# Decode attention: 256 rows of wo loaded to the lower half of the partitions through eight DMA engines, and O turned to match

## The chip, the cores and the metric

One core of one Trainium2 chip. The metric is the device time of one execution, in microseconds (us). Where single executions are compared I also give their span, the time from the first to the last instruction. All runs here are of state fast. The granted clock is the share of TensorE's full clock that the profile records, and half clock is 0.5. SBUF is the on-chip memory in which the tiles here lie, on 128 partitions; PSUM holds TensorE's results (`s_ps`, `acc`). Names: PE is TensorE's matmul, PEld its weight load, DVE VectorE, ACT ScalarE, SPq the queue of SyncE that issues the loads.

## The reference

Attention over a cache for one new token, plus an MLP, on a normalised input:

```python
B, Sq, D = 8, 1, 576;  H, Sk, Dh = 32, 4096, 128;  F = 4608
xn = layernorm(x)
q  = (xn @ wq) as [B, H, 1, Dh]
o  = softmax(q @ k_cache^T * Dh**-0.5) @ v_cache      # caches: 8 x 32 x 4096 x 128, bf16
return x + o as [B, 1, H*Dh] @ wo + gelu(layernorm(xn) @ w1 + b1) @ w2 + b2
```

The two caches are 537 MB; wo is 4096 x 576 (4.7 MB) and w2 is 4608 x 576 (5.3 MB).

## The kernel before

32 tiles of K and 32 of V stream through a ring in SBUF, 8.4 MB each. While the last tile is computed, w2 and then wo are queued behind it. The tail does the second layer of the MLP (`hidden_part`, twice 18 row blocks), turns the attention output into OT, and multiplies it by the 32 rows of wo that each partition holds.

```python
CUTS = (0, 12, 23, 30, RO)                      # RO = 32 rows of wo per partition
...                                             # SyncE, after two blocks of the last K tile
sy.dma_start(out=w2_sb..., in_=w2_v).then_inc(w2_in, 16)
wo_in = []
for n, (r0, r1) in enumerate(zip(CUTS, CUTS[1:])):
    if n == 1:
        sy.wait_ge(sem["kf"], NX * (NT - 1) + 5)
    wo_in.append(nc.alloc_semaphore(f"in_wo{n}"))
    to, rows = wo_rows(r0, r1), wo_v[:, r0 * D:r1 * D]
    sy.dma_start(out=to, in_=rows).then_inc(wo_in[-1], 16)
...                                             # TensorE, the tail
te.wait_ge(w2_in, 16)
hidden_part()                                   # 18 row blocks, two matmuls each (a "pair")
te.wait_ge(sem["on"], NT)
... # 8 matmuls: S_ps[0] <- Ox, low
hidden_part()
te.wait_ge(sem["on"], NT + 1)                   # VectorE has copied OT out of PSUM
for n, (r0, r1) in enumerate(zip(CUTS, CUTS[1:])):
    te.wait_ge(wo_in[n], 16)
    rows = wo_rows(r0, r1).rearrange("p (r d) -> p r d", d=D)
    for r in range(r0, r1):
        ins = accumulate(te, OT[:, r, :], rows[:, r - r0, :], stop=(r == RO - 1))
ins.then_inc(sem["end"], 1)
```

`accumulate` is a pair: two matmuls of 288 columns, into two PSUM banks.

The softmax here doesn't subtract the row's maximum and nothing guards it: scores larger than these inputs give would overflow.

Of the kernel before, what the change touches and what calls it, by code (L numbers as in the profile page):

```python
# [4 lines left out]
ACT = mybir.ActivationFunctionType  # L5
# [3 lines left out]
BF16 = mybir.dt.bfloat16  # L9
P = 128  # L10
# [113 lines left out]
def decode(nc, A_x, A_k_cache, A_v_cache, A_wq, A_wo, B_x, B_w1, B_b1, B_w2, B_b2, out):  # L124
    B, _, D = A_x.shape
# [5 lines left out]
    NT = B * NHG  # L131
# [14 lines left out]
    RO = HD // P  # L146
# [12 lines left out]
    wo_v = A_wo.rearrange("(p r) d -> p (r d)", r=RO)  # L159
    k_v, v_v = (c.rearrange("b h (p c) d -> (b h p) (c d)", p=QP) for c in (A_k_cache, A_v_cache))  # L160

    def sb(name, shape, dtype):
        return nc.alloc_sbuf_tensor(name, list(shape), dtype)

    TILE = 2 * CHUNK
    BLOCK = CB * Dh
    NX = 2 * NCB
    RING = 3 * TILE - BLOCK
    ring = sb("ring", [P, RING], BF16)[:]
# [9 lines left out]
    on = sb("on", [P, G], BF16)  # L179
    fin = sb("fin", [P, ND], BF16)  # L180
    OT = sb("OT", [P, RO, B], BF16)
    hT_sb = sb("hT_sb", [P, R, 2 * B], BF16)
    ident = sb("ident", [P, P], BF16)
    ones_b = sb("ones_b", [1, B], BF16)
# [17 lines left out]
    def early(room, shape, dtype=BF16):  # L202

        n = 2 if dtype == FP32 else 1
        for m in shape[1:]:
            n *= m
        a = rooms[room][0]
        rooms[room][0] = a + (n + 15) // 16 * 16
        assert rooms[room][0] <= rooms[room][1]
        t = ring[:shape[0], a:a + n]  # L210
        if dtype == FP32:
            t = t.bitcast(FP32)
        if len(shape) > 2:
            names = "abcd"[:len(shape) - 1]
            t = t.rearrange(
                f"p ({' '.join(names)}) -> p {' '.join(names)}", **dict(zip(names, shape[1:])))
        return t
# [10 lines left out]
    q = early(0, [P, NB])  # L228
# [10 lines left out]
    S_ps = [s_all[:, i * NB:(i + 1) * NB] for i in range(NS)]  # L239
# [4 lines left out]
    sem = {n: nc.alloc_semaphore(f"m_{n}") for n in names}  # L244
# [23 lines left out]
    def home(t, kind):  # L268

        return 0 if kind else TILE + t % 2 * (TILE - BLOCK)  # L270

    def load_kv(cache, t, kind):
# [10 lines left out]
        out=ident[:], in_=ident[:], compare_op=ALU.not_equal, fill=1.0, base=0,  # L283
# [11 lines left out]
    def act(reads, writes, emit):  # L295
        return od.op("scalar", reads, writes, emit)
# [19 lines left out]
    def spread(src, skey, p0):  # L316
# [5 lines left out]
        out=par2[:], in_=ident[:].rearrange("p (u v) -> p v u", v=2), axis=AX.X, op=ALU.add))  # L322
    dve(["par2"], ["par"], lambda e: e.tensor_copy(
        out=par[:, 0::2], in_=par2[:].unsqueeze(1).to_broadcast([P, (WC + 1) // 2, 2])))
    for v in range(2):
        dve(["par2"], ["par"], lambda e: e.tensor_copy(
            out=par[:, 1::2, v:v + 1],
            in_=par2[:, 1 - v:2 - v].unsqueeze(1).to_broadcast([P, WC // 2, 1])))
# [3 lines left out]
    idn = ident[:]  # L332
# [10 lines left out]
    for t, (dst, dkey) in enumerate(((xT, "xT"), (yT, "yT"))):  # L343
        for v in range(2):
            dve(["tot", "par"], [dkey], lambda e: e.tensor_tensor(
                out=dst[:, :, v * B:(v + 1) * B], in0=tp[:, :, t],
                in1=par[:, :, v:v + 1].to_broadcast([P, WC, B]), op=ALU.mult))
    act(["ident"], ["sel"], lambda e: e.activation(
        func=ACT.Copy, out=sel, in_=idn.rearrange("p (m i) -> p i m", m=M)[:, :2 * B, :].unsqueeze(3)
        .to_broadcast([P, 2 * B, M, QP])))  # L350
    dve(["ident"], ["selc"], lambda e: e.tensor_reduce(
        out=selc[:], in_=idn.rearrange("p (m g c) -> p c g m", m=M, c=4), axis=AX.X, op=ALU.add))
    dve(["ident"], ["headf"], lambda e: e.tensor_reduce(
        out=headf[:], in_=idn.rearrange("p (g q) -> p g q", g=G), axis=AX.X, op=ALU.add))
    act(["headf"], ["head"], lambda e: e.activation(out=head[:], in_=headf[:], func=ACT.Copy))
    with nc.allow_low_precision(reason="zeros and ones"):
        dve(["ident"], ["quad"], lambda e: e.tensor_reduce(
            out=quad[:], in_=idn.rearrange("p (m r) -> p m r", m=M), axis=AX.X, op=ALU.add))
        dve(["ident"], ["low"], lambda e: e.tensor_reduce(
            out=low[:], in_=idn.rearrange("p (m r) -> p r m", m=M), axis=AX.X, op=ALU.add))  # L360
    act(["ident"], ["bv"], lambda e: e.activation(
        func=ACT.Copy, out=bv[:, :2 * B].rearrange("p (v b) -> p v b", v=2),
        in_=ident[:2, :2].unsqueeze(2).to_broadcast([2, 2, B])))


    def queries(e):
        for c in range(WC):
            wv = wq_sb[:, c, :].rearrange("p (x m d) -> p m x d", m=M, d=Dh)
            for m in range(M):
                i = e.matmul(  # L370
                    S_ps[0][m * MP:(m + 1) * MP, :], lhsT=xT[:, c, :], rhs=wv[:, m],
                    start=(c == 0), stop=(c == WC - 1))
        return i

    def accumulate(e, lhsT, rhs, start=False, stop=False):
        for m in range(NO):
            i = e.matmul(  # L377
                acc[m][m * OP:m * OP + B, :ND], lhsT=lhsT, rhs=rhs[:, m * ND:(m + 1) * ND],
                start=start, stop=stop)
        return i  # L380
# [44 lines left out]
    for j in range(HJ):  # L425
        t1, k1, hp, h = t1s[j], f"t1_{j}", h_ps[j], hs[j]
        act(["h_ps"], [k1], lambda e: e.activation(out=t1, in_=hp, func=ACT.Square))  # L427
        dve([k1], [k1], lambda e: e.tensor_scalar(  # L428
            out=t1, in0=t1, scalar1=0.044715, scalar2=1.0, op0=ALU.mult, op1=ALU.add))
# [3 lines left out]
            out=t1, in0=t1, scalar1=1.0, scalar2=0.5, op0=ALU.add, op1=ALU.mult))  # L433
        dve([k1, "h_ps"], [f"h{j}"], lambda e: e.tensor_tensor(
            out=h, in0=t1, in1=hp, op=ALU.mult))
    for j in range(HJ):
        h = hs[j]
        t = S_ps[j][:, :HK * HS * MP].rearrange("p (k n) -> p k n", k=HK)

        def turn(e, h=h, t=t):  # L440
# [8 lines left out]
            out=hT_sb[:].rearrange("p (s j k) n -> p j k s n", s=HS, j=HJ)[:, j],  # L449
            in_=t.rearrange("p k (s n) -> p k s n", s=HS)[:, :, :, :2 * B]))  # L450
# [1 line left out]
    mlp_done = [od.last(e) for e in ("tensor", "vector", "scalar")]  # L452


    CUTS = (0, 12, 23, 30, RO)
    W2_AT = home(NT, 0)
    WO_AT = (W2_AT + 2 * R * D, home(NT - 1, 0))
    assert WO_AT[0] + CUTS[1] * D <= WO_AT[1] and (RO - CUTS[1]) * D <= 3 * BLOCK
    w2_sb = ring[:, W2_AT:WO_AT[0]].rearrange("p (v r d) -> p v r d", v=2, d=D)

    def wo_rows(r0, r1):
        at = WO_AT[0] + r0 * D if r0 < CUTS[1] else WO_AT[1] + (r0 - CUTS[1]) * D
        return ring[:, at:at + (r1 - r0) * D]

    sy = nc.sync
    for token in (wq_read, *head_done):
        od.wait("sync", token)
# [10 lines left out]
    sy.dma_start(out=w2_sb.rearrange("p v r d -> p v (r d)"), in_=w2_v).then_inc(w2_in, 16)  # L478
    wo_in = []
    for n, (r0, r1) in enumerate(zip(CUTS, CUTS[1:])):  # L480
        if n == 1:
            sy.wait_ge(sem["kf"], NX * (NT - 1) + 5)
        wo_in.append(nc.alloc_semaphore(f"in_wo{n}"))
        to, rows = wo_rows(r0, r1), wo_v[:, r0 * D:r1 * D]
        sy.dma_start(out=to, in_=rows).then_inc(wo_in[-1], 16)
    sy.br("sync_end").branch_hint(sync_last)


# [15 lines left out]
    ve, sa, te = nc.vector, nc.scalar, nc.tensor  # L504
# [87 lines left out]
    with nc.Fori(0, NT // 2, 1, engines=[ENG.DVE, ENG.Activation]) as it:  # L592
# [8 lines left out]
    ve.tensor_copy(  # L601
        out=OT[:], in_=S_ps[0][:, :RO * B].rearrange("p (r b) -> p r b", b=B)).then_inc(sem["on"], 1)
    ve.wait_ge(sem["end"], 2)
    ve.tensor_copy(out=fin[:B], in_=acc[0][:B, :ND]).then_inc(fin_d, 1)  # L604
    sa.wait_ge(sem["end"], 2)
    sa.activation(
        out=fin[OP:OP + B], in_=acc[1][OP:OP + B, :ND], func=ACT.Copy).then_inc(fin_a, 1)
    sa.wait_ge(fin_a, 1)
# [34 lines left out]
    def value(name, low, high):  # L643
        return te.snap(regs[name].handles[0], min_val=low, max_val=high)
# [3 lines left out]
    to = s_all[:, bass.ds(value("bank", 0, (NS - 1) * NB), NB)].rearrange("p (c d) -> p c d", d=DL)  # L648
    te.wait_ge(sem["prod"], 1).then_inc(sem["prod"], -1)  # L649
    for d in range(Dh // DL):  # L650
        ins = te.matmul(  # L651
            to, lhsT=idn, rhs=k[:, :, d * DL:(d + 1) * DL], start=(d == 0), stop=(d == Dh // DL - 1))
# [12 lines left out]
    for i, (a, b) in enumerate(groups):  # L665
        te.wait_ge(sem["ebd"], i + 1)
        for j in range(a * J // NCB, b * J // NCB):
            m = j % M
            c = SLOTS[j * NCB // J] * CB + 4 * j % CB
            ins = te.matmul(  # L670
                o_ps[m * MP:(m + 1) * MP, :], lhsT=ebd[:, j].rearrange("p g c -> p (g c)"),
                rhs=vals[:, c:c + 4, :], start=(j < M), stop=(j >= 2 * J - M))
# [4 lines left out]
    for c in range(4):  # L677
        ins = te.matmul(  # L678
            oT_ps[:, :G], lhsT=ob[:, c, :], rhs=selc[:, c, :], start=(c == 0), stop=(c == 3))
# [20 lines left out]
    for b in range(B):  # L700
        ins = te.matmul(  # L701
            ot[:, :, b], lhsT=Ox[:, b * NHG:(b + 1) * NHG].rearrange("p n g m -> p (n g m)"),
            rhs=low[:], start=True, stop=True)
# [1 line left out]
    hidden_part()  # L705
    assert not parts
    te.wait_ge(sem["on"], NT + 1)
    for n, (r0, r1) in enumerate(zip(CUTS, CUTS[1:])):
        te.wait_ge(wo_in[n], 16)
        rows = wo_rows(r0, r1).rearrange("p (r d) -> p r d", d=D)  # L710
        for r in range(r0, r1):
            ins = accumulate(te, OT[:, r, :], rows[:, r - r0, :], stop=(r == RO - 1))
    ins.then_inc(sem["end"], 1)
# [28 lines left out]
```

## Time and profile before

| | before |
|---|---|
| device time, median of 3 (range) | 1292.88 us (1292.68 to 1293.12) |
| span of the profiled execution | 1291.5 us |
| w2 landed | 1277.82 us |
| wo loads landed | 1281.97, 1285.75, 1288.18, 1288.88 us |
| last matmul ends | 1289.56 us |

Two lines of the profile's table of 40 equal slices, one digit for each slice. The DMA engines are busy at nine tenths or more in 39 of 40: the body is a stream of loads, and nothing in this change touches it.

```profile
PEclk8778887778887777887777887778887777888778
DMA  9999999999999999999999999999999999999998
```

The end of the chain of waits (start us, length us, what). Read it upwards: the store waits for VectorE, VectorE for TensorE, and TensorE started when w2 landed. wo is not in it.

```profile
1252.92 24.91 DMA ring<-in_B_w_dram
1277.83 0.04 issue
1277.87 4.49 PE acc L377 x36
1282.36 0.54 PE s_ps L701 x8
1282.90 6.68 PE acc L377 x100
1289.58 0.03 issue
1289.60 0.45 DVE fin L604
```

The same stretch in the timeline (start, busy us, engine, line, operation). Each group of matmuls starts as the last one ends: TensorE has no gap.

```profile
1277.87 4.49 PE L377 MATMUL acc<-ring,hT_sb 128*8 128x288 bf16 x36 [2.77 <-DMA ring<-in_B_w_dram]
...
1282.29 0.61 PE L701 MATMUL s_ps<-low,Ox 128*128 128x32 bf16 x8
...
1282.83 2.81 PE L377 MATMUL acc<-ring,hT_sb 128*8 128x288 bf16 x36
...
1285.47 4.09 PE L377 MATMUL acc<-ring,OT 128*8 128x288 bf16 x64
```

The first 36 hidden matmuls take 4.49 us and the next 36 only 2.81. The busy time by stretch says why: the number before the last two in a row is the granted TensorE clock. It is 0.50 up to 1283.8 us and 1.00 after. The clock records put the fall at 1276.94 us. Each of this execution's 69 clock records but the last, which is cut off, lasts a multiple of 3.413 us (this half clock 6.83 us), so the changes lie on one grid.

```profile
1277.00:1280.40 3.40, 2.53 (x22) 1.41 (x24) 0.00 (x0) 0.00 (x0) 0.00 (x0) 0.50 0.99 421
1280.40:1283.80 3.40, 3.40 (x36) 1.79 (x32) 0.42 (x1) 0.00 (x0) 0.00 (x0) 0.51 0.99 419
1283.80:1287.00 3.20, 3.20 (x56) 2.31 (x54) 0.00 (x0) 0.00 (x0) 0.00 (x0) 1.00 0.95 394
```

The loads of the tail, from the view of DMA issues (KB, us from issue to landing):

```profile
ring<-in_B_w_dram SPq DMA_DIRECT2D x1, 5184.0 KB, 24.9
ring<-in_A_wo_dram SPq DMA_DIRECT2D x1, 1728.0 KB, 28.6
ring<-in_A_wo_dram SPq DMA_DIRECT2D x1, 1584.0 KB, 26.5
ring<-in_A_wo_dram SPq DMA_DIRECT2D x1, 1008.0 KB, 28.5
ring<-in_A_wo_dram SPq DMA_DIRECT2D x1, 288.0 KB, 28.7
```

A load counts as landed when all sixteen of its completion increments have come. The trace records when each comes, but not from which engine. The profile counts 16 DMA engines, and I take each increment as one engine's. For the last wo load of before, in us after the first increment:

```
1287.06 + 0  .01 .15 .20 .23 .30 .39 .41 .42 .45 .47 .62 .67 .94 | 1.78 1.83
```

Fourteen come within 0.94 us, two are 0.84 and 0.89 us behind the last of these, and the load counts as late as the last. Two are late nearly all along. Before's packets show two 16 KB instruction fetches, at 30 and 76 us, about 1.02 us each. The two loads that landed before the first (at 13.6 and 25.9 us) have all sixteen increments within 0.77 us. At the first tile after the first fetch (44.5 us) one increment is 1.24 us behind the fourteenth, and at every tile from 83 us on two are, by 1.09 to 1.16 us.

### The profile page before, as it was taken

The page shows a single profiled execution, that of the slowest core. Times are in us where ns is not written, and L with a number is a line of the kernel's source. Part 1 is how long each engine was busy: PE and PEld are TensorE (multiplying, and loading weights), DVE is VectorE, ACT ScalarE, POOL GpSimd, SP SyncE. Part 2 cuts the span into 40 slices and gives each one's busy share as a digit, 9 for nine tenths or more (in the row PEclk, how much of TensorE's full clock was granted, in tenths as well). Part 3 has the DMA queues.
Part 4 walks back from the last instruction along what each step waited for, and adds up shares of the span by engine and source line. Part 5 has one row for each costly group of instructions (what it writes and reads, how often), then busy time and mean ns, then how long its engine had stood idle before and what let it go on. Part 6 is the DMA issues. An engine that isn't in the chain of part 4 may idle for free. (4 is left out here: it accounts for less than half of the span.)

```text
span 1291.5 us, 14664 instructions
## 1 busy us (share of the span) xinstructions
PE 734.5 (57%) x4707; PEld 321.8 (25%) x4707; DVE 829.2 (64%) x740; ACT 56.7 (4%) x181; POOL 2.4 (0%) x12
## 2 busy tenths in 40 slices
PE   4654565554565554565554565554566554565557
PEld 1222232222222222222222232222222222222223
DVE  2655677655677655677655677655677655577654
ACT  2000000000000000000000000000000000000000
POOL 0000000000000000000000000000000000000000
PEclk8778887778887777887777887778887777888778
DMA  9999999999999999999999999999999999999998
GB/s 421 440 425 436 436 426 447 426 426 449 424 426 451 422 428 449 422 430 447 422 438 438 426 436 436 426 445 428 426 447 426 426 449 424 426 451 422 430 447 348
DMA packets 10409, 557.00 MB, mean 431 GB/s; under 512 B 1163, under 2 KB 1188, under 8 KB 1446
## 3 DMA queue, kind: packets, MB, share of 16 engines
q1 hardware_dynamic: 10368, 556.93, 99.7%
q8 instruction: 2, 0.03, 0.0%
q10 hardware_dynamic: 38, 0.02, 0.0%
q14 instruction: 1, 0.01, 0.0%
HBM read 556.94 MB, written 0.01 MB: 431 GB/s over the span
## 5 line engine op out<-in xcount | busy, mean ns | idle before, releaser
L651 PE MATMUL s_ps<-ring,ident 128*128 x2048 | 541.1, 421 | 517.4 <-PEq L649 516.9
L559 DVE TENSOR_TENSOR ring<-ring,qb 128x4096 bf16<-128x4096 bf16 x256 | 578.9, 2282 | 281.8 <-DMA ring<-in_A_k_cache_dram 281.5
L651 PEld LDWEIGHTS s_ps<-ring,ident 128*128 128x128 bf16 x2048 | 216.4, 106 | 829.3 <-issue 678.7
L534 DVE TENSOR_REDUCE sc<-s_ps 128x32 f32<-128x512 f32 x256 | 171.3, 682 | 0.0
L670 PE MATMUL o_ps<-ring,ebd 128*32 128x512 bf16 x2048 | 116.4, 380 | 0.0
L546 DVE TENSOR_TENSOR ebd<-es,head 128x1536 bf16<-128x1536 bf16 x64 | 77.8, 1216 | 0.0
L569 DVE RECIPROCAL rec<-tot_ps 128x8 f32<-128x8 f32 x32 | 6.6, 207 | 110.8 <-PE oT_ps L678 110.8
L582 ACT ACTIVATE es<-sc 128x192 bf16<-128x192 f32 x64 | 19.8, 310 | 1104.2 <-DVE sc L534 1104.2
L670 PEld LDWEIGHTS o_ps<-ring,ebd 128*32 128x32 bf16 x2048 | 51.6, 97 | 62.6 <-issue 13.6
L678 PE MATMUL oT_ps<-selc,ob 128*128 128x8 f32 x256 | 33.9, 259 | 12.3 <-ACT ob L586 12.3
L678 PEld LDWEIGHTS oT_ps<-selc,ob 128*128 128x128 f32 x256 | 31.0, 191 | 15.2 <-ACT ob L586 15.2
L586 ACT ACTIVATE ob<-o_ps 128x512 f32<-128x512 f32 x32 | 19.1, 597 | 80.3 <-PE o_ps L670 80.3
L428 DVE TENSOR_SCALAR ring<-ring 96x384 f32<-96x384 f32 x2 | 0.7, 352 | 26.5 <-ACT ring L427 26.5
L545 DVE TENSOR_TENSOR Es<-Ep 128x1 f32<-128x1 f32 x32 | 5.1, 160 | 13.3 <-ACT es L582 13.3
L674 PEld LDWEIGHTS tot_ps<-headf,Es 128*128 128x128 f32 x64 | 9.5, 187 | 13.6 <-issue 13.6
L674 PE MATMUL tot_ps<-headf,Es 128*128 128x8 f32 x64 | 12.4, 266 | 0.0
L582 ACT ACTIVATION_READ_ACCUMULATOR es<-sc 128x1 f32 x64 | 11.9, 186 | 0.0
L417 PE MATMUL o_ps<-ring 128*32 128x384 bf16 x27 | 7.9, 861 | 2.9 <-DMA ring<-in_B_w_dram 2.9
L574 DVE TENSOR_TENSOR Ox<-on,quad 128x32 bf16 x32 | 6.2, 192 | 4.8
L377 PE MATMUL acc<-ring,hT_sb 128*8 128x288 bf16 x72 | 7.3, 381 | 2.8 <-DMA ring<-in_B_w_dram 2.8
L417 PE MATMUL s_ps<-ring 128*32 128x384 bf16 x27 | 7.9, 863 | 0.0
L339 PE MATMUL tot_ps<-ident,ring 40*128 40x16 bf16 x9 | 0.7, 206 | 11.6 <-DVE ring L317 11.6
(76 smaller groups left out, 61.5 us busy)
## 6 DMA issues: line engine op xcount, KB each, us to landing
ring<-in_B_w_dram SPq DMA_DIRECT2D x2, 5184.0 KB, 25.2
ring<-in_A_wq_dram SPq DMA_DIRECT2D x1, 4608.0 KB, 13.7
ring<-in_A_wo_dram SPq DMA_DIRECT2D x1, 1728.0 KB, 28.6
ring<-in_A_wo_dram SPq DMA_DIRECT2D x1, 1584.0 KB, 26.5
ring<-in_A_wo_dram SPq DMA_DIRECT2D x1, 1008.0 KB, 28.5
ring<-in_A_k_cache_dram SPq DMA_DIRECT2D x32, 31.9
ring<-in_A_v_cache_dram SPq DMA_DIRECT2D x32, 30.5
ring<-in_A_wo_dram SPq DMA_DIRECT2D x1, 288.0 KB, 28.7
```

The source lines that it names most:

```text
L377: i = e.matmul(acc[m][m * OP:m * OP + B, :ND], lhsT=lhsT, rhs=rhs[:, m * ND:(m + 1) * ND], start=start, stop=stop)
L417: i = e.matmul(h_ps[j][s * MP:(s + 1) * MP], lhsT=lhsT, rhs=wv[:, r0:r0 + HK, :], **flags)
L534: ins = ve.tensor_reduce(out=sc[:, n * CB:(n + 1) * CB], in_=bank_of(x).rearrange("p (c d) -> p c d", d=DL), axis=AX.X, op=ALU.add)
L546: ve.tensor_tensor(out=ebd[:, ja:jb], in0=es[:, a:b].rearrange("p (j c) -> p j c", c=4).unsqueeze(2) .to_broadcast([P, nj, G, 4]), in1=hea ...
L559: ve.tensor_tensor(out=k, in0=k, in1=qb[:, bass.ds(t, 1), :].to_broadcast([P, CB, Dh]), op=ALU.mult,).then_inc(sem["prod"], 1)
L569: ve.reciprocal(out=rec[:], in_=tot_ps[:, :G]).then_inc(sem["rec"], 1)
L582: sa.activation(out=es[:, a * CB:b * CB], in_=sc[:, a * CB:b * CB], func=ACT.Exp, scale=scale, accum_out=Ep[:, i:i + 1]).then_inc(sem["x"], 1)
L586: sa.activation(out=ob[:].rearrange("r c d -> r (c d)"), in_=o_ps, func=ACT.Copy).then_inc(sem["ob"], 1)
L651: ins = te.matmul(to, lhsT=idn, rhs=k[:, :, d * DL:(d + 1) * DL], start=(d == 0), stop=(d == Dh // DL - 1))
L670: ins = te.matmul(o_ps[m * MP:(m + 1) * MP, :], lhsT=ebd[:, j].rearrange("p g c -> p (g c)"), rhs=vals[:, c:c + 4, :], start=(j < M), stop ...
L674: te.matmul(tot_ps[:, :G], lhsT=Es[:].to_broadcast([P, P]), rhs=headf[:], start=True, stop=True).then_inc(sem["vf"], 1)
L678: ins = te.matmul(oT_ps[:, :G], lhsT=ob[:, c, :], rhs=selc[:, c, :], start=(c == 0), stop=(c == 3))
```

## The change

Intent: the two laggards seem to be among eight DMA engines that I call the upper ones. So two of the 32 wo rows of each partition, 256 of 4096 rows, leave the common load. They go to partitions 0 to 63, by intent through the other eight, the lower engines, in four loads of 72 KB; the upper engines have less to do and should finish sooner. The diff is cut. The rows then lie on other partitions than the O values they belong to, so TensorE multiplies O by a permuted identity (`turned`), VectorE copies the result (`OL`), and the products run at half height, four pairs instead of two.

```diff
+    NE, NJ = 8, 4
+    turned = sb("turned", [P, P], BF16)          # ScalarE fills it in the prologue (cut)
+    OL = sb("OL", [P // 2, 2, 2, B], BF16)
-    CUTS = (0, 12, 23, 30, RO)
+    SHIFT = 2
+    CUTS = (0, SHIFT, 11, 23, 30, RO)
+    HOMES = 11
...
+        for h in range(2):
+            for q in range(0, PL, NE * NJ):       # PL = 64
+                in_ = wo_v[PL * h + q:PL * h + q + 1, r0 * D:r1 * D]
+                sy.dma_start(
+                    out=low_rows[q:q + NE * NJ, h * SHIFT * D:(h + 1) * SHIFT * D],
+                    in_=bass.AP(in_.tensor, in_.offset,
+                        [[RO * D, NE], [NE * RO * D, NJ], [1, SHIFT * D]])).then_inc(wo_in[-1], 16)
...
     te.wait_ge(sem["on"], NT + 1)
-    for n, (r0, r1) in enumerate(zip(CUTS, CUTS[1:])):
+    for h in range(2):
+        ins = te.matmul(S_ps[1][:PL, h * SHIFT * B:(h + 1) * SHIFT * B],
+            lhsT=turned[:, h * PL:(h + 1) * PL],
+            rhs=OT[:, :SHIFT].rearrange("p r b -> p (r b)"), start=True, stop=True)
+    ins.then_inc(sem["end"], 1)                   # VectorE: OL <- S_ps[1]
+    for n in (1, 0, *range(2, len(wo_in))):
+        r0, r1 = CUTS[n], CUTS[n + 1]
+        if not n:
+            te.wait_ge(sem["on"], NT + 2)
+            te.wait_ge(wo_in[n], 16 * 2 * PL // (NE * NJ))
+            for h in range(2):
+                for r in range(SHIFT):
+                    at = (h * SHIFT + r) * D
+                    accumulate(te, OL[:, h, r, :], low_rows[:, at:at + D])
+            continue
         te.wait_ge(wo_in[n], 16)
```

More of the change, by code (lines that the diff above doesn't have):

```diff
@@ L363, in decode @@
         in_=ident[:2, :2].unsqueeze(2).to_broadcast([2, 2, B])))
+    act(["ident"], ["turned"], lambda e: e.activation(
+        func=ACT.Copy, out=turned[:].rearrange("p (q e j) -> p q e j", e=NE, j=NJ),
+        in_=idn.rearrange("p (q j e) -> p q e j", e=NE, j=NJ)))
     def queries(e):
@@ L452, in decode @@
     mlp_done = [od.last(e) for e in ("tensor", "vector", "scalar")]
-    CUTS = (0, 12, 23, 30, RO)
+    SHIFT = 2
+    CUTS = (0, SHIFT, 11, 23, 30, RO)
+    HOMES = 11
     W2_AT = home(NT, 0)
     WO_AT = (W2_AT + 2 * R * D, home(NT - 1, 0))
-    assert WO_AT[0] + CUTS[1] * D <= WO_AT[1] and (RO - CUTS[1]) * D <= 3 * BLOCK
+    assert WO_AT[0] + (SHIFT + HOMES) * D <= WO_AT[1] and (RO - HOMES) * D <= 3 * BLOCK
     w2_sb = ring[:, W2_AT:WO_AT[0]].rearrange("p (v r d) -> p v r d", v=2, d=D)
     def wo_rows(r0, r1):
-        at = WO_AT[0] + r0 * D if r0 < CUTS[1] else WO_AT[1] + (r0 - CUTS[1]) * D
+        at = WO_AT[0] + (SHIFT + r0) * D if r0 < HOMES else WO_AT[1] + (r0 - HOMES) * D
         return ring[:, at:at + (r1 - r0) * D]
+    PL = P // 2
+    low_rows = ring[:PL, WO_AT[0]:WO_AT[0] + 2 * SHIFT * D]
     sy = nc.sync
@@ L480, in decode @@
     for n, (r0, r1) in enumerate(zip(CUTS, CUTS[1:])):
-        if n == 1:
+        if r0 == HOMES:
             sy.wait_ge(sem["kf"], NX * (NT - 1) + 5)
         wo_in.append(nc.alloc_semaphore(f"in_wo{n}"))
-        to, rows = wo_rows(r0, r1), wo_v[:, r0 * D:r1 * D]
-        sy.dma_start(out=to, in_=rows).then_inc(wo_in[-1], 16)
+        if r1 > SHIFT:
+            sy.dma_start(out=wo_rows(r0, r1), in_=wo_v[:, r0 * D:r1 * D]).then_inc(wo_in[-1], 16)
+            continue
[4 more added lines that the diff above has]
+                    out=low_rows[q:q + NE * NJ, h * SHIFT * D:(h + 1) * SHIFT * D],
+                    in_=bass.AP(
+                        in_.tensor, in_.offset,
+                        [[RO * D, NE], [NE * RO * D, NJ], [1, SHIFT * D]])).then_inc(wo_in[-1], 16)
     sy.br("sync_end").branch_hint(sync_last)
@@ L603, in decode @@
     ve.wait_ge(sem["end"], 2)
+    ve.tensor_copy(
+        out=OL[:].rearrange("p h r b -> p (h r b)"), in_=S_ps[1][:PL, :2 * SHIFT * B]
+    ).then_inc(sem["on"], 1)
+    ve.wait_ge(sem["end"], 3)
     ve.tensor_copy(out=fin[:B], in_=acc[0][:B, :ND]).then_inc(fin_d, 1)
-    sa.wait_ge(sem["end"], 2)
+    sa.wait_ge(sem["end"], 3)
     sa.activation(
@@ L707, in decode @@
     te.wait_ge(sem["on"], NT + 1)
-    for n, (r0, r1) in enumerate(zip(CUTS, CUTS[1:])):
+    for h in range(2):
+        ins = te.matmul(
+            S_ps[1][:PL, h * SHIFT * B:(h + 1) * SHIFT * B], lhsT=turned[:, h * PL:(h + 1) * PL],
+            rhs=OT[:, :SHIFT].rearrange("p r b -> p (r b)"), start=True, stop=True)
[9 more added lines that the diff above has]
+                    accumulate(te, OL[:, h, r, :], low_rows[:, at:at + D])
+            continue
         te.wait_ge(wo_in[n], 16)
```

## The prediction

What the sum used was my assumption: eight engines, called lower, share the 128 packets of the four loads (2304 B, two rows of 1152 B), 16 each. "The clock's phase" means where the clock's changes fall against w2's landing. The sum reads: the lower engines +1.44 - 0.69 = +0.75 us, the upper ones -0.69 us, so -0.1 to -0.4 us on the bound of the loads and +0.35 us on TensorE's, tied before at 1292.88 us. It came to 1292.9 us.

> **What bounds the kernel now.** The page's table of slices shows the sixteen DMA engines busy at nine tenths or more in almost every slice, 431 GB/s over the span: until the last weights are on their way it is a DMA stream. Only the tail can change. The chain of waits gives it: w2 lands at 1277.83 us, then 36 + 8 + 100 matmuls on TensorE to 1289.57, the DVE cast, and the store. In the timeline TensorE has no gap there: pairs of 288-column matmuls start every 240 ns up to 1283.77 and every 122.5 ns after (the clock records say 0.5, then 1.0). The loads of wo are nearly as late: 1281.97, 1285.75, 1288.18, 1288.88. TensorE reaches the third at 1288.17 (its weight load waits about 50 ns for it) and the fourth at 1289.03, 0.15 us after it landed. So TensorE and DMA finish the tail almost tied: landing of the third + 9 pairs x 0.1225 + about 0.2 us = 1289.5.
>
> The sixteen completion increments of each load show why DMA is late: fourteen engines finish within 0.7 to 0.96 us, two are about 0.85 us behind the rest. The packets show two 16 KB instruction fetches, at 30 and 76 us, about 1.02 us each, after which those two lag for good. Following packets end to start, both seem to be engines of the upper half.
>
> **The change.** 256 of 4096 rows (295 KB) leave the common load. [...] A 2304-byte packet takes 93 ns (about 0.09 us apart), so lower engines gain 16 x 0.09 = 1.44 us and lose 18.4 KB, 0.69 us: +0.75 net. Upper engines lose 0.69. The laggards then end the last load near 1288.2, the lower ones at 1288.4 to 1288.8; the third load lands near 1287.8 to 1288.1. The DMA floor of the tail falls by 0.1 to 0.4 us.
>
> It adds to TensorE: two turning matmuls (about 0.05 us each, as the eight of L701, plus a change of shape: 0.12 us together) and half-height products, 4 row pairs instead of 2: +0.245 us. About +0.35 us on an engine with no gap. The DVE copy (about 0.3 us) hides behind nine rows (1.1 us) that TensorE takes first. The ScalarE copy in the prologue and three more DMA issues are off the path. w2, which starts the tail, is untouched.
>
> So -0.1 to -0.4 on one bound, +0.35 on the other, tied before. Which binds depends on how long TensorE runs at half clock after w2: 5.9 us here. [...]
>
> **Prediction: 1292.9 us, range 1292.4 to 1293.5.** Faster by over 2%: 1%; within: 98%; slower: 1%.
>
> **Right if** the last wo load lands 0.1 to 0.6 us sooner with its sixteen increments closer together; TensorE does not wait for any wo load; its tail from w2's landing is about 0.35 us longer at the same half-clock time. **Wrong if** the laggards sit in the lower half (last landing 0.7 us later, +0.7 us), the four loads use all engines, the clock's phase or an instruction fetch moves, or TensorE waits for the DVE copy.

## The result and the profile after

| | before | after |
|---|---|---|
| device time, median of 6 (range) | 1292.88 us (1292.68 to 1293.91) | 1293.24 us (1292.53 to 1294.05) |
| w2 landed, in the profile | 1277.82 | 1277.88 |
| last two full-height wo loads landed | 1288.18, 1288.88 | 1287.92, 1288.60 |
| last matmul ends | 1289.56 | 1289.23 |

The ratio is 1.0002, with an interval of 0.9989 to 1.0015: the same time. A ratio is the mean time of one kernel's fast runs over that of the other's of the same rounds, so it is not quite the ratio of the medians above. The best of these six runs of the change is below the best of before's six, and its worst above the worst of before's six; 27 further runs of before, below, reach 1294.14.

Chain of waits, after. L384 is before's L377, L728 before's L701; L736 is the turning.

```profile
1252.97 24.91 DMA ring<-in_B_w_dram
1277.88 0.04 issue
1277.92 4.04 PE acc L384 x36
1281.97 0.34 PE s_ps L728 x8
1282.31 2.30 PE acc L384 x36
1284.61 0.16 PE s_ps L736 x2
1284.77 4.48 PE acc L384 x68
1289.25 0.02 issue
1289.27 0.44 DVE fin L631
```

Timeline, after. Follow the starts from 1284.54: turning, nine pairs, VectorE's copy beside them, four half-height pairs, and the rest.

```profile
1284.54 0.23 PE L736 MATMUL s_ps<-OT,turned 128*64 128x16 bf16 x2
...
1284.70 1.27 PE L384 MATMUL acc<-ring,OT 128*8 128x288 bf16 x18
1284.81 0.18 DVE L627 CAST OL<-s_ps 64x32 bf16<-64x32 f32 x1 [2.03 <-PE s_ps L736]
...
1285.90 0.65 PE L384 MATMUL acc<-ring,OL 64*8 64x288 bf16 x8
...
1286.48 2.75 PE L384 MATMUL acc<-ring,OT 128*8 128x288 bf16 x42
```

Stretches, after. The clock (0.66, then 0.84) is higher than before's 0.50 and 0.51 in the same stretches. The clock records give 3.41 us at half clock after w2 landed, against 5.90 us in before's profile. The change did not do that: w2 lands at the same time, and TensorE's work up to that point is unaltered.

```profile
1277.00:1280.40 3.40, 2.48 (x23) 1.43 (x24) 0.00 (x0) 0.00 (x0) 0.00 (x0) 0.66 1.04 438
1280.40:1283.80 3.40, 3.40 (x50) 2.25 (x48) 0.42 (x1) 0.00 (x0) 0.00 (x0) 0.84 0.99 420
1283.80:1287.00 3.20, 3.20 (x52) 1.88 (x48) 0.18 (x1) 0.00 (x0) 0.00 (x0) 1.00 0.88 365
```

Loads, after (the line x4 has no time to landing because its four loads share a semaphore):

```profile
ring<-in_A_wo_dram SPq DMA_DIRECT2D x1, 1008.0 KB, 28.2
ring<-in_A_wo_dram SPq DMA_DIRECT2D x4, 72.0 KB
ring<-in_A_wo_dram SPq DMA_DIRECT2D x1, 288.0 KB, 28.4
```

The increments of the last wo load, after:

```
1286.37 + 0  .15 .16 .19 .26 .67 | 1.61 1.72 1.75 1.77 1.85 1.86 1.87 1.92 2.10 2.24
```

For w2, which the change does not touch, the same execution has offsets 0 .15 .16 .17 .22 .25 .29 .29 .38 .40 .45 .67 .69 .76 and 1.76 1.88. The records do not name the engines, but the offsets match: six kept the small offsets (0 to .67), two kept 1.76 and 1.88 (now 1.77 and 1.87), and eight moved back together by about 1.45 us against the rest. The eight that moved are those that took the extra loads, so both laggards are among the other eight, and the last to finish are now engines with the extra loads. These I call the lower ones. From w2 to the last load the first upper engine took 10.36 us, against 11.07 before, 0.71 us less; the lower ones took about 0.74 us more.

To compare TensorE's tail between executions I take out the clock. From the first hidden matmul to the end of the last matmul, less half of the half-clock time in it, before is 11.69 - 5.90/2 = 8.74 us and after is 11.30 - 3.41/2 = 9.60 us. This is rough, because not everything doubles at half clock: from the pair before the eight `S_ps` matmuls to the pair after them took 0.92 us at half clock in before and 0.56 at full clock in after.

### The profile page after: what moved, and what is told of

Read it like the earlier page. It is cut to its first block, busy times and chain, and to the rows that moved or that the text cites. A ratio compares the mean times of both kernels' runs of the same rounds, so it can differ in the third digit from the quotient of the medians.

```text
span 1291.2 us, 14682 instructions
## 1 busy us (share of the span) xinstructions
PE 733.1 (57%) x4713; PEld 321.9 (25%) x4713; DVE 829.6 (64%) x741; ACT 56.9 (4%) x182; POOL 2.4 (0%) x12
## 5 line engine op out<-in xcount | busy, mean ns | idle before, releaser
L701 PEld LDWEIGHTS tot_ps<-headf,Es 128*128 128x128 f32 x64 | 9.5, 186 | 13.6 <-issue 13.6
L701 PE MATMUL tot_ps<-headf,Es 128*128 128x8 f32 x64 | 12.4, 266 | 0.0
L384 PE MATMUL acc<-ring,hT_sb 128*8 128x288 bf16 x72 | 6.4, 349 | 2.8 <-DMA ring<-in_B_w_dram 2.8
```

Of the source, the lines that this page charges most:

```text
L384: i = e.matmul(acc[m][m * OP:m * OP + B, :ND], lhsT=lhsT, rhs=rhs[:, m * ND:(m + 1) * ND], start=start, stop=stop)
L701: te.matmul(tot_ps[:, :G], lhsT=Es[:].to_broadcast([P, P]), rhs=headf[:], start=True, stop=True).then_inc(sem["vf"], 1)
```

## The experiments

**The theory.** The tail has two bounds, nearly tied in before. The load bound is the landing of the last wo loads plus the pairs that follow. The TensorE bound is w2's landing, plus 8.74 us, plus half of a half-clock time that varies between executions. The change lowers the first and raises the second, so it makes the best executions better, the worst worse, and leaves the median.

**Rivals.** A: the loads are no bound at all, only the clock moves the time. B: the loads are the only bound, and TensorE's extra work is free.

Beside the twelve runs, before ran 27 times on the same chips. Its spans have a median of 1291.6 us and lie between 1291.3 and 1292.8, 24 of 27 at or below 1291.8. The change's six spans are 1291.2, 1291.2, 1291.3, 1291.9, 1292.1, 1292.5. That is the pattern the theory asks for: three at or below before's least, three above 1291.8. None of those three was traced, and their mean clocks (0.812, 0.815, 0.816) are not below those of the other three (0.812, 0.814, 0.816).

I use spans because in some executions, of eight of the thirteen kernels, before among them, the device time exceeds the span by 2.0 to 2.6 us instead of the usual 1.3 to 1.6. Four of five executions of the kernel "split" below were of this kind, and the median of its device times (1294.05) is mostly that. What happens there lies outside the first and last instruction, and I did not settle it.

### dma_only: the loads of the change without its extra work (wrong result)

```diff
-    for h in range(2):
-        ins = te.matmul(S_ps[1]..., lhsT=turned..., ...)      # and VectorE's copy of OL
...
-            for h in range(2):
-                for r in range(SHIFT):
-                    accumulate(te, OL[:, h, r, :], low_rows[:, at:at + D])
+            for r in range(SHIFT):
+                accumulate(te, OT[:, r, :], ring[:, WO_AT[0] + r * D:WO_AT[0] + (r + 1) * D])
```

> Wrong result on purpose: the four lower-half loads are made as in the change, but TensorE multiplies the first two rows as in the kernel before (one full-height pair each, no turning, no copy). Theory (two nearly tied bounds): TensorE's tail is 8.7 us at full clock plus half of its half-clock time, as before; the third and fourth load of full rows land at 1287.9 and 1288.6 us instead of 1288.18 and 1288.88, so the last matmul ends at 1289.3 us where the half-clock time is short and at 1289.6 or later where it is long: 0 to 0.3 us less than before, best run 0.25 us below the best of before. Rival A (the loads are no bound at all, only the clock's phase moves the time): the same times as before within 0.1 us, best run included. Rival B (loads are the only bound): every run 0.27 us less.

Measured: 1292.60 us median (1292.51 to 1293.75). Spans 1291.2, 1291.2, 1291.3, 1292.2, 1292.4. The last load landed at 1288.64 us and the third full-height one at 1287.95. In its profile, with 3.33 us of half clock, the chain of waits no longer starts at w2. It goes through a wo load, and TensorE waited for it:

```profile
1259.76 28.19 DMA ring<-in_A_wo_dram
1287.95 0.04 issue
1288.00 1.29 PE acc L384 x18
```

Nine pairs after that landing come to 1289.27 us, as expected (1289.3), and three of five spans are 0.3 us or more below before's median of 1291.6. That speaks against A. B wanted every execution lower, but two are at 1292.2 and 1292.4. The theory does not reach them either: with the longest half-clock record in any of these tails (6.83 us) TensorE would end at 1277.9 + 8.74 + 3.41 = 1290.06, a span of about 1292.0. So this kernel, without the extra work on TensorE, shows nearly the change's pattern: three executions at 1291.3 or less, two at 1292.2 or more. That the loads themselves bring long executions is a rival that no run settles, since neither of these two was traced. The comparison with the reference passed for this kernel and the next although both are wrong in two rows of wo, so a passed comparison is no proof of these rows.

### pe_only: the extra work without the loads (wrong result)

```diff
+    # turned, OL, the two turning matmuls and VectorE's copy as in the change
     for n, (r0, r1) in enumerate(zip(CUTS, CUTS[1:])):          # before's CUTS and loads
         te.wait_ge(wo_in[n], 16)
+        if n == 0:      # rows 2..10, then four half-height pairs, then row 11
+            ...accumulate(te, OL[:, h, r, :], rows[:PL, r, :])
```

> Wrong result on purpose: the loads of the kernel before, with the change's extra work on TensorE and VectorE (two turning matmuls, copy, eight half-height matmuls in place of four full ones). Theory: loads land as before (last at 1288.88), TensorE's tail at full-clock equivalent rises from 8.74 to about 9.6 us as in the change, so it ends between 1289.5 (short half-clock time, bound by loads) and 1290.8; median 0.3 to 0.6 us above before and 0.3 or more above the variant with the loads alone. Rival B (loads are the only bound): as before within 0.1 us. My prediction's size of the extra work (0.35 us) would give 9.1 us.

Measured: 1293.09 us median (1292.76 to 1293.67). Spans 1291.4, 1291.7, 1291.7, 1291.8, 1292.3, median 0.1 us above before. The profiled execution is the one at 1292.3. It had 5.58 us of half clock, and its chain runs from w2 through TensorE alone to 1290.37:

```profile
1278.13 4.48 PE acc L383 x36
1282.61 0.54 PE s_ps L711 x8
1283.15 2.59 PE acc L383 x36
1285.74 0.16 PE s_ps L719 x2
1285.90 4.47 PE acc L383 x68
```

The tail without the clock is 12.23 - 5.58/2 = 9.43 us: 0.69 us more than before, twice what I predicted. So the extra work is not free in this execution (against B). The median moved by less than the 0.3 to 0.6 us that I expected. By the theory the load bound hides the work where the half-clock time is short; the other four executions were not traced.

### split and split_lower: w2 in two halves

```diff
-    sy.dma_start(out=w2_sb..., in_=w2_v).then_inc(w2_in, 16)
+    for v in range(2):
+        sy.dma_start(out=w2_sb[:, v]..., in_=w2_v[:, v]).then_inc(w2_in[v], 16)
...
+    te.wait_ge(w2_in[1], 16)
     hidden_part()                               # the second half
```

In before, half clock begins within TensorE's wait of 2.77 us for w2; here TensorE is to start before such a wait.

> The kernel before with w2 loaded as two halves, each with its own semaphore, so that TensorE starts the first half at about 1275.2 us, straight after the last tile, and need not cool down. Theory: TensorE stops being a bound; the last matmul ends 1.38 us after the third wo load lands, at 1289.55 us, in every run: best run as before, spread between runs under 0.3 us instead of 0.4 to 1.2, no long half-clock stretch after 1277 us. If the waits between the wo loads let the clock fall to half, the last nine pairs take 2.2 instead of 1.1 us and it is 0.5 to 1.1 us slower. Rival A (phase of the clock alone, loads no bound): about 1.5 us or more faster.

> The change with w2 split in the same way. Theory: with TensorE early, what the lower-half loads give at the DMA shows: last wo load at about 1288.6, third at 1287.9, last matmul at 1289.3, 0.2 to 0.3 us less than the split kernel without the change, and 0.2 to 0.9 less than the change alone; if the clock falls to half in the waits, the gain is lost in part. Rival A: the extra work on TensorE is still paid in full, 0.3 to 0.9 us more than the split kernel without the change.

Measured: split, on before, 1294.05 us median; spans 1291.5, 1291.6, 1291.7, 1292.1, 1292.3. split_lower, on the change, 1293.32 us; spans 1291.3, 1291.5, 1291.8, 1292.0, 1292.7. The spread did not shrink. TensorE now sits in the wo loads' waits (1.86 and 2.05 us in split), and the clock fell again: split_lower's profile has half clock from 1284.94 to 1288.35, within the wo rows. This was the alternative written beside the expectation. In that trace it cost the gain: the last matmul ended at 1289.57, not the expected 1289.3. split_lower is no better than split in the median (1291.8 against 1291.7), and the comparison of the two decides nothing. A is out: in split's profile TensorE started 2.7 us earlier (1275.18 us), the clock stayed full throughout, and still the last matmul ended at 1289.63, against 1289.56 in before. Its chain goes through the third wo load:

```profile
1259.82 28.50 DMA ring<-in_A_wo_dram
1288.32 0.04 issue
1288.36 1.29 PE acc L377 x18
```

### warm, warm_lower, warm_fine, warm_lower_fine: hold the clock up

Dummy matmuls into the free bank `o_ps` fill TensorE's waits. In the two "fine" kernels the last cuts of wo are 28 and 31 rows instead of 30, so that four pairs and one pair follow the last two landings instead of nine and two. All four are meant to compute the right result.

```diff
+    def keep_warm(n):
+        for _ in range(n):
+            te.matmul(o_ps, lhsT=idn, rhs=qb[:, :4].rearrange("p t d -> p (t d)"), start=True, stop=True)
+    keep_warm(12)
     te.wait_ge(w2_in, 16)
...
+        keep_warm(...)    # warm: 6, 4 before the 2nd, 3rd load; warm_fine: 6, 1;
+                             # warm_lower: 2, 3 before the 2nd, 3rd full-height load; warm_lower_fine: 2, 0
         te.wait_ge(wo_in[n], 16)
...
-    CUTS = (0, 12, 23, 30, RO)                  # on the change: (0, 2, 11, 23, 30, RO)
+    CUTS = (0, 12, 23, 28, 31, RO)              # fine; on the change (0, 2, 11, 23, 28, 31, RO)
```

What the theory tests is whether the half-clock time in the tail makes the spread.

> The kernel before, with dummy matmuls into a free PSUM bank in TensorE's waits (12 before w2, 6 and 4 before the second and third wo load; 0.22 us each at full clock). Right result. Theory [...]: no half-clock stretch after 1270 us, TensorE reaches every wo load early, the last matmul ends 1.38 us after the third wo load lands, 1289.5 us, in every run; the times shrink to about the best of before, median 1292.7, spread under 0.4 us. Rival (the spread comes from elsewhere, the DMA or the launch): spread as before, 0.4 to 1.2 us; if the dummies only cost, 0.5 us or more slower.

> The change, with dummy matmuls in the waits (12, 2, 3). Theory: TensorE's extra 0.7 us is off the path, the DMA gain of the lower-half loads is what remains: last matmul at 1289.3 us, median 1292.45, 0.25 us below the same dummies without the change. Rival (the loads give nothing): the same as the dummies without the change, or slower.

> Dummies as in the first kernel of this call, and the wo loads cut at 28 and 31 rows instead of 30, so that fewer row pairs (4, then 1) follow the last two landings. Theory: the last matmul ends about 0.45 us after the last load's landing at 1288.9, so 1289.35 us, 0.2 us less than with dummies alone; median 1292.5.

> The change with dummies and the finer cuts. Theory: both gains add: last load at 1288.6, last matmul at 1289.05 us, median 1292.2, 0.7 us or more below the medians of before and of the change, spread under 0.4 us. If the extra TensorE work still binds, no better than the finer cuts without the change.

| spans, us, in order | loads as before | loads of the change |
|---|---|---|
| dummies | 1291.6 1291.6 1291.6 1291.7 1293.1 | 1291.0 1291.3 1291.3 1291.3 1292.4 |
| dummies, finer cuts | 1291.1 1291.2 1291.2 1291.5 1291.5 | 1290.8 1290.9 1290.9 1291.0 1292.1 |
| last matmul ends: dummies | 1289.60 | 1289.33 |
| last matmul ends: dummies, finer cuts | 1289.09 | 1288.86 |

The "finer" row also has fewer dummies than the row above it, so what the cuts alone give is not read from this table. In device time the medians are 1293.88 (warm), 1292.63 (warm_lower), 1292.56 (warm_fine) and 1292.38 us (warm_lower_fine). The first is 1.2 us over what I expected, although four of its spans agree within 0.1 us: two of the five executions have the long time outside the span, and one a long span. The other three are 0.06 to 0.18 us over. In none of the four profiles is there any half clock between w2's landing and the last matmul. With TensorE out of the way, the loads of the change are worth 0.3 us in both rows of medians (1291.6 to 1291.3, 1291.2 to 1290.9), where they were worth nothing in the change alone. The spread of most executions shrank, but three of the four kernels have one execution 1.1 to 1.4 us above the rest. Its mean clock (0.815 to 0.818) is not below the others', so the clock is not shown to be its cause; none of these was traced.

### shift1, wlf_again, fine, fine_lower

```diff
# shift1: warm_lower_fine with one row per partition through the lower engines
-    SHIFT = 2
+    SHIFT = 1
# wlf_again: warm_lower_fine once more.   fine, fine_lower: before and after with the finer cuts, no dummies
```

> The change with dummies and finer cuts, but one row per partition (128 rows of wo, 147 KB) through the lower engines instead of two. Theory of balance: the two lagging upper engines lose 0.35 us, the lower ones gain about 0.4 us and now stay behind the laggards; last wo load lands at 1288.6 us, as with two rows (1288.53 in its trace) and 0.35 us before the mean of full-height loads (1288.95); TensorE does two half-height pairs less. Span median 1290.9 us, as with two rows. Rival (the gain grows with the bytes moved): 1288.8 us landing, span 0.15 to 0.2 us more than with two rows.

> A repeat of the change with dummies and finer cuts, for its time and for another trace. Span median 1290.9 us, at least 0.5 us below before's 1291.6; four of five executions within 0.3 us.

> The kernel before with the finer cuts alone, no dummies, loads on all partitions. Theory of two bounds: the load bound falls by 0.2 us but TensorE's stays, so only executions with a short half-clock time gain: best span 1291.1 to 1291.2, median 1291.4, spread as before or larger. Rival (the load bound alone counts): all executions at 1291.1 to 1291.2.

> The change with the finer cuts, no dummies. Theory: the load bound is lowest, 1290.9 us of span, but TensorE's extra 0.7 us makes it bind in most executions: span between 1290.9 and 1292.4, median 1291.4 to 1291.8, no better than before; with the dummies it was 1290.9 in four of five. Rival (the extra work is off the path): median 1290.9.

| | spans, us, in order | device time, median |
|---|---|---|
| shift1 | 1290.8 1290.8 1291.1 1291.5 1292.0 | 1292.43 |
| wlf_again | 1290.7 1290.9 1291.0 1291.0 1291.0 | 1292.36 |
| fine | 1291.2 1291.3 1291.4 1291.4 1291.9 | 1293.01 |
| fine_lower | 1290.8 1291.0 1292.2 1292.2 1292.3 | 1293.49 |

fine_lower looks like both bounds at once. Without dummies two executions reach the load bound (1290.8 and 1291.0, the same as wlf_again), and three are at 1292.2 or more. The two have a mean clock of 0.812, the three of 0.811. With the dummies it was 1291.0 or less in nine of ten executions (warm_lower_fine and wlf_again), which agrees with the extra work binding where TensorE has not been kept at full clock. It is not shown: the three long executions were not traced, and a mean clock lower by 0.001 over the whole span does not say where in the span it was lower. My expectation for its median (1291.4 to 1291.8) was too low: it is 1292.2. fine, with before's work on TensorE, came out as expected (best 1291.2, median 1291.4). The chain of waits of wlf_again ends in a wo load and four pairs, and nothing of TensorE before them is in it:

```profile
1260.04 28.32 DMA ring<-in_A_wo_dram
1288.36 0.04 issue
1288.40 0.68 PE acc L384 x8
```

When the last wo load landed, over all traces:

| | traces | mean | range, us |
|---|---|---|---|
| loads as before | 6 | 1288.98 | 1288.74 to 1289.13 |
| two rows by the lower engines | 7 | 1288.58 | 1288.38 to 1288.71 |
| one row (shift1) | 1 | 1288.49 | |

The gain of the loads is 0.40 us, and the ranges do not meet. Half the bytes gave as much, which is what balance predicts and "the more the better" does not. With one row the upper laggards are still last (the two are 1.49 and 1.67 us after the first engine, against 1.53 and 1.69 at w2; the eight that moved are at 0.92 to 1.34). With two rows lower engines are last. This rests on one trace, and shift1's median span (1291.1) is 0.2 us over what I expected, through two long executions.

**A kernel with a lower median than both.** The change with dummies and finer cuts has a median of 1292.37 us over ten executions, against 1292.98 us for 27 of before: 0.6 us, or 0.05%. Seven of the ten are at or below 1292.48, under the best of before's 27 (1292.68). The two ratios, 0.9996 and 0.9997, have intervals that include 1 (0.9982 to 1.0010 and 0.9984 to 1.0011). shift1 does nearly as well with half the turned rows.

## Why the prediction was right or wrong

**The total, 1292.9 us in a range of 1292.4 to 1293.5: right** (1293.24). The number proves little: the range holds before's own 1292.88, so no effect at all would have met it too, and the medians of the spans are the same (1291.6). Of the reason, a lower load bound against a higher TensorE bound that were tied, each part was seen in a trace: the load bound in dma_only, the TensorE bound in pe_only, and the load gain in the warm kernels. In after's own profile they are tied again: the third full-height load at 1287.92 plus nine pairs (1.31 us) is 1289.23, where TensorE ended. That the TensorE bound makes the change's long executions is argued, not shown. That the median fell inside the range although the TensorE term was half its true size is partly luck.

**The engines: right.** "Both seem to be engines of the upper half": the increments of after split into six and two that kept their offsets and eight that moved. That the four loads go through eight engines, and through those without the laggards, was my assumption; the trace agrees, since exactly eight engines took about 0.74 us longer and the two laggards are not among them. Their numbers no run here shows. "+0.75" and "-0.69" against 0.74 and 0.71.

**"The DMA floor of the tail falls by 0.1 to 0.4 us": right.** It is 0.28 us between the two profiles, 0.40 between the means of 6 and 7 traces.

**"About +0.35 us on an engine with no gap": wrong by half.** It measured 0.69 us in pe_only, whose eight `S_ps` matmuls ran at half clock as before's did. The 0.86 us between before and after contains the roughness told above. Between the starts of after's pairs, the turning took 0.378 us where the next pair would have followed in 0.1225, so 0.26 us instead of my 0.12. The four half-height pairs took 0.80 us where two full ones and the step to the next would have taken 0.37, so 0.43 instead of 0.245. Together that is 0.69 as well. The mis-sized term is the change of the matmul's shape. The first matmul after three of the four changes started 0.212 to 0.216 us after the last of the old shape, where the next pair usually follows in 0.12 (the fourth, from turning back to pairs, took 0.106). I had allowed for one such change and for none at the half-height pairs. Here three of the four cost about 0.09 us each. What TensorE does in that time no run here shows.

**"With its sixteen increments closer together": wrong.** The spread grew from 1.83 to 2.24 us, because the upper engines that had been early became earlier still. Only the last one counts.

**"TensorE does not wait for any wo load": nearly.** In after's profile it reached the third full-height load as it landed (1287.92, weight load at 1287.96), and the pair came about 0.01 us late.

**The phase of the clock as the cause of the spread: shown in part.** The phase differs between the two traces: half clock begins 0.88 us before w2 lands in before (1276.94 us) and 0.21 us after it in after (1278.09 us), and in after too each complete clock record lasts a multiple of 3.413 us. The half-clock time after w2 was 2.88 to 5.90 us in six traces without dummies or a split w2, whose w2 landings lie within 0.26 us of each other. That agrees with a phase that differs between executions; what sets it no run shows. But with dummies to hold the clock up single executions, none of them traced, still lay 1.1 to 1.4 us above the rest at mean clocks no lower, so something else seems to add to the spread. What stays open is that and the extra 1 us or so outside the span.

## What to carry to other kernels

When two engines finish a stage almost tied, a change that moves work from one to the other can leave the median where it was, as here; test each half alone, take the other bound away before judging it, and trace a long execution as well as a short one. A DMA load was as late here as the last of its sixteen increments (in before 0.89 us behind the fourteenth). Moving a few rows to the early engines can gain what the late ones lose, no more: two rows took 0.71 us from the late ones and brought the last landing forward by 0.40 us, and one row, in a single trace, did as much. So move the least that does it. Count a change of matmul shape as work of its own (about 0.09 us at three of four here), and look for waits that let TensorE's clock fall (before's fell in a wait of 2.77 us; with dummies in it, none of four profiles has half clock in the tail) before counting its time at full speed.
